# A state-space layer and a routed MLP on one core: statistics made in fours, a copy moved to VectorE, neighbours reordered

## The chip, the cores and the metric

One core of a Trainium2 chip runs one program. The metric is device time in microseconds of one execution; the time of a kernel is the median of its runs. The engines are named as in the profile: PE (TensorE), DVE (VectorE), ACT (ScalarE), POOL (GpSimd), SP (SyncE, which issues most transfers).

## What is computed

`x` is 2048 tokens by 1024, bf16. With `xn` the layer norm of `x`, the output is `x + A(xn) + B(xn)`:

```python
# A: diagonal complex state space, 1024 states
Lam_bar = exp(dt * Lam);  B_bar = ((Lam_bar - 1) / Lam)[:, None] * Bmat
Bu = einsum("bld,pd->blp", x, B_bar)
h = Lam_bar * h + Bu[:, t, :]                 # over all tokens t
y = 2 * einsum("blp,dp->bld", hseq, Cmat).real + x * Dskip
# B: the two tokens with the largest x @ w_r go through a gated MLP (1024 -> 3584 -> 1024)
out = x + scatter_add(zero, idx, ((silu(x_sel @ w_gate) * (x_sel @ w_up)) @ w_down) * sigmoid(r_sel))
```

In A and B, `x` stands for `xn`; B's own `x` is `xn` too. So the output holds `x + xn + Dskip * xn` besides the two products, and as `x = std * xn + mean`, the kernel makes it as `(Dskip + std + 1) * xn + mean`. That is where the standard deviations and means of the title are used.

## The kernel before, in words

The 2048 tokens are cut into 16 chunks of 128, frames of two chunks and superframes of four. A chunk `c` goes through these tasks:

- `x.c` loads it (SP). For chunks 0 to 5 the statistics are `bs.c`, `bn.c` on DVE (L317, L320) and `nmean.c` on POOL; for chunks 6 to 15 `sum.c`, `nmean.c`, `sq.c` on ACT (L326, L357, L332). `rstd.c` on ACT is a logarithm (L283), an Exp for 1/std (L284) and an Exp for std (L286). `apply.c` normalizes, on DVE for chunks 0 to 5 (L346) and on ACT from 6 on (L350). `nmr.c` is minus the mean times 1/std, `nmr1.c` adds one to std (L360 on POOL, L369 on ACT), `mean.c` turns the sign of the negated mean (L363, POOL).
- `Tpe.c` turns the normalized chunk by eight PE transposes (L386, chunks 0 to 3) and `xnT.c` copies it from PSUM (L391 DVE, L393 ACT); from chunk 4 on `T.c` is a transposed transfer.
- `Bu.f.j`, in the first frames split into `Bh.f.j.ri`, multiplies frame `f` by block `j` of B, real and imaginary (L661); `Bs.s.j.ri` does it for a superframe (L672). Block 0 of B is turned by PE (`tB.ri`, L262) and copied by ACT (`B.0.ri`, L265); the others come as transposed transfers (`B.j.ri`, L240). The products go to three PSUM banks in turn, from which ACT evacuates them (`u`, L667; `us`, L680).
- `TI` turns the input by a phase (DVE, L738 to L747), `SC` scans (DVE, L766), `gb` casts the scan (ACT, L772), `cw`, `cy`, `cin` carry the state from chunk to chunk (POOL), `TO` turns back (DVE).
- `xr.c` loads `x` again, `seed.c.dh` puts half `dh` of `xn` into a PSUM bank (ACT, L871), `sk.c.dh` multiplies it by `Dskip + std + 1` (DVE, L881), `Y.c.q` adds the output projection (PE, L891), `ADD.c.dh` adds the mean and evacuates (ACT, L907; DVE for chunk 15, L905), `out.c.dh` stores.
- The MLP: weights by SP (`w.n`), products by PE (`mm.i`), the two rows added to chunk 15's bank by PE where they belong there (`hotY`, L896) and scattered into the output by an indirect transfer (`fix`, L1136).

At the start `warm.i` runs matmuls on the identity (L409, L305) until data is there.

The order of the work is written out by hand: `ORDER` (L25 to L68) lists the tasks, and `Plan.emit` issues them in that order. Each engine then works through its own instructions in order, and waits by semaphores. `Plan.run` only asserts that each task's dependences and buffers stand ahead of it; the durations given to `add` set nothing here.

## Time and profile before

| | us |
|---|---|
| median of 3 runs | 250.15 (250.13 to 250.19) |
| the profiled execution | 250.2 |
| its span, first to last instruction | 248.1 |
| PE busy | 241.1 (97%) |
| DVE busy | 231.0 (93%) |
| ACT busy | 177.4 (71%) |
| POOL busy | 92.1 (37%) |
| mean granted TensorE clock | 0.998 |

The profiled execution is some 2 us longer than its span, for what lies before the first and behind the last instruction. A busy share is an average over the whole span; DMA-issuing instructions are not in it. Rows of a timeline give the start and the busy time; neighbouring instructions of one engine overlap a little, so the start of the next is often before the end of the row above.

### The profile page before, as it was taken

To read this page: it belongs to the slowest core of one execution; us is meant where nothing else is said; L and a number is where in the kernel's file an instruction comes from. 1 tells how busy PE (TensorE), PEld (TensorE's weight loads), DVE (VectorE), ACT (ScalarE), POOL (GpSimd) and SP (SyncE) were. 2 spreads that over 40 slices of the span, in tenths; PEclk is the share of its full clock that TensorE was granted. 3 is DMA by queue.
4 is the path that set the end of the run, shared out by engine and by line. 5 is a ranking of instruction groups with operands and counts; after the bars stand their busy time and mean duration, and the time that the engine had idled before them with its cause. 6 is when DMAs were issued, how large, how long until landed. Compare 5 with 4: busy or idle time off the path is not lost.

```text
span 248.1 us, 4602 instructions
## 1 busy us (share of the span) xinstructions
PE 241.1 (97%) x1723; PEld 139.9 (56%) x1743; DVE 231.0 (93%) x267; ACT 177.4 (71%) x364; POOL 92.1 (37%) x148
## 2 busy tenths in 40 slices
...
GB/s 206 237 190 150 210 171 249 144 274 131 237 144 109 106 97 114 127 3 10 118 184 248 165 0 116 393 225 320 274 176 400 251 376 340 281 202 391 66 64 44
DMA packets 66753, 46.77 MB, mean 189 GB/s; under 512 B 46114, under 2 KB 52648, under 8 KB 66732
## 3 DMA queue, kind: packets, MB, share of 16 engines
...
q8 instruction: 13, 0.21, 0.3%
q10 hardware_dynamic: 192, 0.07, 0.1%
q14 instruction: 8, 0.07, 0.1%
...
## 4 chain that ended last, share of the span: by engine, by line
PE 94%; DMA 2%; issue 1%; DVE 1%; SPq 1%
PE pY L891 44%; PE pB L661 23%; PE pB L672 22%; PE pG L1086 3%; DMA xt<-in_A_x_dram 2%; PE pD L1117 1%; PE r_ps L404 1%; DVE ot L905 1%; PE pT L386 1%; SPq L180 0%; SPq L168 0%; DVE xn L346 0%; SPq L169 0%; PE pY L896 0%; PE pP L474 0%
## 5 line engine op out<-in xcount | busy, mean ns | idle before, releaser
L891 PE MATMUL pY<-CT,hT 128*128 128x512 bf16 (+1 forms) x515 | 113.1, 372 | 0.9 <-issue 0.3
L891 PEld LDWEIGHTS <-hT 128*128 128x128 bf16 x528 | 51.2, 98 | 58.9 <-issue 1.9
L766 DVE TENSOR_TENSOR_SCAN gf<-R,v 128x1040 f32<-128x1040 f32 (+1 forms) x34 | 68.9, 2055 | 1.4 <-POOL v L798 1.0
L782 POOL TENSOR_TENSOR cw<-gf,tL 128x16 f32<-128x16 f32 (+1 forms) x34 | 33.4, 984 | 97.5 <-DVE gf L766 89.8
L672 PE MATMUL pB<-xnT,BT 128*128 128x512 bf16 x249 | 57.0, 379 | 0.4
L661 PE MATMUL pB<-xnT,BT 128*128 128x256 bf16 (+1 forms) x576 | 57.3, 261 | 0.0
L661 PEld LDWEIGHTS <-BT 128*128 128x128 bf16 x576 | 51.1, 98 | 5.6
L907 ACT ACTIVATE ot<-pY,mean_all 128x512 bf16<-128x512 f32 x30 | 20.5, 686 | 33.4 <-PE pY L891 33.2
L672 PEld LDWEIGHTS <-BT 128*128 128x128 bf16 x256 | 24.8, 98 | 30.4 <-PE pG L1086 0.4
L772 ACT CAST gb<-gf 128x1024 bf16<-128x1024 f32 (+1 forms) x34 | 31.8, 940 | 7.5 <-DVE gf L766 7.3
L808 DVE TENSOR_TENSOR m<-gb,E 128x4096 bf16<-128x4096 bf16 x13 | 29.5, 2271 | 0.5 <-ACT gb L772 0.5
L680 ACT CAST u<-pB 128x256 bf16<-128x256 f32 x64 | 19.9, 376 | 10.0 <-PE pB L672 8.0
L871 ACT ACTIVATE pY<-xr,nmr_all,rstd_all 128x512 f32<-128x512 bf16 (+1 forms) x33 | 25.2, 770 | 0.3
L881 DVE SCALAR_TENSOR_TENSOR pY<-Drow,std_all,pY 128x512 f32<-128x512 bf16 (+1 forms) x33 | 23.5, 723 | 0.6 <-ACT pY L871 0.6
L667 ACT CAST u<-pB 128x512 bf16<-128x512 f32 x32 | 18.2, 578 | 2.1 <-PE pB L661 2.0
L810 DVE TENSOR_TENSOR hT<-m 128x2048 bf16<-128x2048 bf16 x13 | 15.9, 1225 | 1.2
L740 DVE TENSOR_TENSOR v<-u,m 128x4096 bf16<-128x4096 bf16 x7 | 16.0, 2292 | 0.2
L738 DVE TENSOR_TENSOR m<-u,E1t 128x4096 bf16<-128x4096 bf16 x7 | 16.0, 2283 | 0.0
L798 POOL TENSOR_TENSOR v<-cy,v 128x16 bf16<-128x16 f32 (+1 forms) x17 | 14.2, 837 | 1.4
L350 ACT ACTIVATE xn<-xt,nmr_all,rstd_all 128x1024 bf16<-128x1024 bf16 x10 | 12.4, 1238 | 0.1
L332 ACT ACTIVATE xn<-xt,nmean_all 128x1024 bf16<-128x1024 bf16 x10 | 11.5, 1153 | 0.1
L797 POOL CAST v<-cy 128x16 bf16<-128x16 f32 (+1 forms) x17 | 10.4, 610 | 0.8
...
## 6 DMA issues: line engine op xcount, KB each, us to landing
...
```

The costliest lines, as they stand in the source:

```text
L661: nc.tensor.matmul(out=pB[:, ri, ts_], lhsT=BT[ri][j][:, k, :], rhs=xnT_frame(f)[:, k, ts_], start=(k == 0), stop=(k == DT - 1))
L667: nc.scalar.copy(out=u_tiles[f][:, :, :, j, :].rearrange("p c i t -> p i c t"), in_=pB_tiles.pop((f, j))[:].rearrange("p i (c t) -> p i c ...
L672: nc.tensor.matmul(out=pB[:], lhsT=BT[ri][j][:, k, :], rhs=xnT_tiles[s][:, k, :], start=(k == 0), stop=(k == DT - 1))
L680: nc.scalar.copy(out=u_tiles[f][:, :, ri, j, :], in_=pB[:, i * TF:(i + 1) * TF].rearrange("p (c t) -> p c t", c=CPF))
L766: nc.vector.tensor_tensor_scan(out=flat(gf), data0=flat(R[:, js, :]), data1=flat(v[:, ri, js, :]), initial=0.0, op0=ALU.mult, op1=ALU.add)
L772: nc.scalar.copy(out=gb_tiles[c][:, ri, js, :], in_=gf_tiles[c, js.start, ri][:, :, 2:])
L782: nc.gpsimd.tensor_tensor(out=cw_tiles[c, js.start][:, ri, :, 0:n], in0=g.unsqueeze(1).to_broadcast([128, 2, n]), in1=tL[:, ri, :, js], op ...
L808: nc.vector.tensor_tensor(out=m[:].rearrange("p k i j t -> p k (i j t)"), in1=E2[:].rearrange("p k i j t -> p k (i j t)"), in0=flat(gb[:]) ...
L871: nc.scalar.activation(out=pY[:, 0:d_.stop - d_.start], in_=y_tiles["xr", c][:, d_], func=ACT.Identity, bias=nmr_all[:, c:c + 1], scale=rs ...
L881: nc.vector.scalar_tensor_tensor(out=pY, in0=ms["Drow"][:, d_], scalar=std1_all[:, c:c + 1], in1=pY, op0=ALU.add, op1=ALU.mult)
L891: nc.tensor.matmul(out=pY, lhsT=h_tiles[c][:, ri, j, :], rhs=CT[ri][h][:, j, d0:d0 + w], start=False, stop=end, skip_group_check=True)
L907: nc.scalar.activation(out=ot, in_=pY, func=ACT.Identity, bias=mean_all[:, c:c + 1])
```

## The change

Three things are changed in the code, and the order besides. The standard deviation is no longer made with each `rstd`: the logarithms are kept in one tile, and `std.g` makes four deviations in one Exp on ACT; `nmr1.g` and `mean.g` are one POOL operation for four chunks each (the additions that ACT did for chunks 6 to 15 go to POOL). `sk` and `ADD` wait for the group's operation. Turned chunk 1 is copied by DVE.

```diff
-    def inv_sqrt(out_ap, var_ap, npart, scale, std=None):
+    def inv_sqrt(out_ap, var_ap, npart, scale):
...
-        if std is not None:
-            nc.scalar.activation(out=std, in_=lv[:npart], func=ACT.Exp, scale=0.5)
...
     def ln_rstd(c, scale):
-        inv_sqrt(rstd_all[:, c:c + 1], ln_part[c][:, 1:2], 128, scale, std1_all[:, c:c + 1])
+        nc.scalar.activation(out=lv_all[:, c:c + 1], in_=ln_part[c][:, 1:2], func=ACT.Ln, bias=eps_t[:], scale=scale)
+        nc.scalar.activation(out=rstd_all[:, c:c + 1], in_=lv_all[:, c:c + 1], func=ACT.Exp, scale=-0.5)
+
+    def ln_std(g):
+        nc.scalar.activation(out=std1_all[:, 4 * g:4 * g + 4], in_=lv_all[:, 4 * g:4 * g + 4], func=ACT.Exp, scale=0.5)
...
-    def ln_std1(c):
-        nc.gpsimd.tensor_scalar_add(out=std1_all[:, c:c + 1], in0=std1_all[:, c:c + 1], scalar1=1.0)
-
-    def ln_mean(c):
-        nc.gpsimd.tensor_scalar_mul(out=mean_all[:, c:c + 1], in0=nmean_all[:, c:c + 1], scalar1=-1.0)
+    def ln_std1(g):
+        nc.gpsimd.tensor_scalar_add(out=std1_all[:, 4 * g:4 * g + 4], in0=std1_all[:, 4 * g:4 * g + 4], scalar1=1.0)
+
+    def ln_mean(g):
+        nc.gpsimd.tensor_scalar_mul(out=mean_all[:, 4 * g:4 * g + 4], in0=nmean_all[:, 4 * g:4 * g + 4], scalar1=-1.0)
...
-    def ln_std1_act(c):
-        nc.scalar.activation(out=std1_all[:, c:c + 1], in_=std1_all[:, c:c + 1], func=ACT.Identity, bias=one_t[:])
...
-    DVE_T = (0,)
+    DVE_T = (0, 1)
...
+    for g in range(NSF):
+        four = range(4 * g, 4 * g + 4)
+        add(("std", g), "ACT", 0.2, lambda g=g: ln_std(g), [("rstd", c) for c in four] + [("log",)], key=4 * g - 24)
+        add(("nmr1", g), "POOL", 0.3, lambda g=g: ln_std1(g), [("std", g)], key=4 * g - 24)
+        add(("mean", g), "POOL", 0.3, lambda g=g: ln_mean(g), [("nmean", c) for c in four], key=4 * g - 24)
```

`ORDER` is another text from its first line on. Two of its first lines, before and after:

```diff
-warm.13 warm.14 tB.0 start.0 nmean.1 x.2 B.1.0 x.3 Tpe.0 Bn.1 B.1.1 B.0.0 xnT.0 bs.2 rstd.1 apply.1 tB.1 Bh.0.0.0 Tpe.1 x.5 bn.2 bs.3 B.0.1 nmean.0
-xnT.1 bn.3 rstd.2 B.2.0 Bh.0.0.1 pP.0 pcol.0 Bh.0.1.0 apply.2 rstd.3 dt frq x.4 B.3.0 B.2.1 Bu.0.0 u.0.0 Bh.0.1.1 Tpe.2 rad Bu.0.1 apply.3 xnT.2 Tpe.3
...
+warm.9 warm.10 warm.11 warm.12 warm.13 warm.14 Tpe.0 xnT.0 Bn.1 x.3 nmean.1 B.1.0 B.1.1 bs.2 apply.1 tB.0 bn.2 tB.1 B.0.0 B.0.1 x.4 Tpe.1 Bh.0.0.0
+B.2.0 B.2.1 B.3.0 rstd.2 xnT.1 bs.3 Bh.0.0.1 pP.0 Bu.0.0 pcol.0 apply.2 x.5 B.3.1 bn.3 dt u.0.0 rstd.3 apply.3 B.4.0 B.4.1 Bh.0.1.0 Tpe.2 Bh.0.1.1
```

Line numbers move by a few: L386 becomes L385, L661 L662, L680 L681, L907 L908.

What PE does at the start, after the last matmul on the identity. Each row is the first matmul of eight; a number behind a name tells buffers apart. Before, with `Bn` the untouched block 0 of B, `xn_185` chunk 0, `xn_240` chunk 1, and `BT0_0`, `BT1_0` the real and imaginary half of block 0:

```order
L262 MATMUL pT_206<-ident_92,Bn_87 128x128
L386 MATMUL pT_221<-ident_92,xn_185 128x128
L262 MATMUL pT_242<-ident_92,Bn_87 128x128
L661 MATMUL pB_251<-xnT_232,BT0_0_115 128x128
L386 MATMUL pT_260<-ident_92,xn_240 128x128
L661 MATMUL pB_251<-xnT_232,BT1_0_123 128x128
L474 MATMUL pP_295<-ident_92,prow_83 128x32
```

After, with `xn_179` chunk 0 and `xn_228` chunk 1:

```order
L385 MATMUL pT_210<-ident_92,xn_179 128x128
L262 MATMUL pT_230<-ident_92,Bn_87 128x128
L262 MATMUL pT_242<-ident_92,Bn_87 128x128
L385 MATMUL pT_255<-ident_92,xn_228 128x128
L662 MATMUL pB_264<-xnT_219,BT0_0_115 128x128
L662 MATMUL pB_264<-xnT_219,BT1_0_123 128x128
L475 MATMUL pP_289<-ident_92,prow_83 128x32
```

Chunk 0 is turned ahead of both halves of B, and the first product stands behind the turn of chunk 1.

VectorE in the same place, from the copy of turned chunk 0 on. Before:

```order
L391 COPY xnT<-pT 128x8x128
L317 BN_STATS st<-xt 128x6
L346 TENSOR_SCALAR xn<-xt,mv,rstd_all 128x1024
L317 BN_STATS st<-xt 128x6
L320 BN_AGGR mv<-st 128x2
L317 BN_STATS st<-xt 128x6 x2
L320 BN_AGGR mv<-st 128x2
L477 CAST pcol<-pP 128x32
L346 TENSOR_SCALAR xn<-xt,mv,rstd_all 128x1024
```

After:

```order
L390 COPY xnT<-pT 128x8x128
L315 BN_STATS st<-xt 128x6
L348 TENSOR_SCALAR xn<-xt,mv,rstd_all 128x1024
L315 BN_STATS st<-xt 128x6
L318 BN_AGGR mv<-st 128x2
L390 COPY xnT<-pT 128x8x128
L315 BN_STATS st<-xt 128x6
L478 CAST pcol<-pP 128x32
L348 TENSOR_SCALAR xn<-xt,mv,rstd_all 128x1024
```

The copy of chunk 1 stands behind the statistics of chunk 2, and one half of chunk 3's statistics goes behind the normalization of chunk 2.

ACT in superframe 2, up to the evacuation of the third group (`us.2.1.0`, the last row of each). Before:

```order
L332 ACTIVATE xn,sm<-xt,nmean_all 128x1024
L357 ACTIVATE nmean_all<-sm 128x1
L871 ACTIVATE pY<-xr,nmr_all,rstd_all 128x512
L283 ACTIVATE lv<-sm,eps_t 128x1
L284 ACTIVATE rstd_all<-lv 128x1
L286 ACTIVATE std_all<-lv 128x1
L680 CAST u<-pB 128x2x128 x2
L871 ACTIVATE pY<-xr,nmr_all,rstd_all 128x512
L680 CAST u<-pB 128x2x128 x2
L907 ACTIVATE ot<-pY,mean_all 128x512
L772 CAST gb<-gf 128x1024
L680 CAST u<-pB 128x2x128 x2
```

After:

```order
L324 ACTIVATE xn,sm<-xt 128x1024
L352 ACTIVATE xn<-xt,nmr_all,rstd_all 128x1024
L681 CAST u<-pB 128x2x128 x2
L872 ACTIVATE pY<-xr,nmr_all,rstd_all 128x512
L773 CAST gb<-gf 128x1024
L681 CAST u<-pB 128x2x128 x2
L773 CAST gb<-gf 128x1024
L908 ACTIVATE ot<-pY,mean_all 128x512
L359 ACTIVATE nmean_all<-sm 128x1
L681 CAST u<-pB 128x2x128 x2
```

The normalization of a chunk (15) and a second cast of the scan now stand ahead of the third evacuation.

## Rows read from the trace of the kernel before

**Rows 1.** The page, part 1: busy us, share of the span, instructions of each engine

```profile
PE 241.1 (97%) x1723; PEld 139.9 (56%) x1743; DVE 231.0 (93%) x267; ACT 177.4 (71%) x364; POOL 92.1 (37%) x148
```

**Rows 2.** PE's waits: line, what it waited for, us in total, times, longest

```profile
PE pT L386 <- DVE xn L346: 0.9, 1, 0.9
PE pT L262 <- DMA Bn<-in_A_B_im_dram: 0.3, 1, 0.3
```

**Rows 3.** PE's timeline: start us, busy us, line, operation, count [idle before it <- releaser]

```profile
1.37 1.89 PE L409 MATMUL warm<-ident 128*128 128x128 bf16 x16 [1.37 <-POOL ident masks.py:199]
...
5.23 0.62 PE L262 MATMUL pT<-ident,Bn 128*128 128x128 bf16 x8
5.74 0.62 PE L386 MATMUL pT<-ident,xn 128*128 128x128 bf16 x8
6.69 0.62 PE L262 MATMUL pT<-ident,Bn 128*128 128x128 bf16 x8 [0.32 <-DMA Bn<-in_A_B_im_dram]
7.14 0.61 PE L661 MATMUL pB<-xnT,BT 128*128 128x128 bf16 x8
8.70 0.62 PE L386 MATMUL pT<-ident,xn 128*128 128x128 bf16 x8 [0.94 <-DVE xn L346]
...
9.81 2.10 PE L661 MATMUL pB<-xnT,BT 128*128 128x128 bf16 x32
11.76 0.61 PE L386 MATMUL pT<-ident,xn 128*128 128x128 bf16 x8
```

**Rows 4.** VectorE's timeline, same columns

```profile
6.45 0.64 DVE L391 COPY xnT<-pT 128x1024 bf16<-128x1024 bf16 x1
7.50 0.69 DVE L317 BATCH_NORM_STATS2 st<-xt 128x6 f32<-128x512 bf16 x1 [0.41 <-DMA xt<-in_A_x_dram]
8.11 0.53 DVE L346 TENSOR_SCALAR xn<-xt,mv,rstd_all 128x1024 bf16<-128x1024 bf16 x1
...
9.28 0.21 DVE L320 BATCH_NORM_AGGREGATE mv<-st 128x2 f32<-128x12 f32 x1
...
11.67 0.17 DVE L486 TENSOR_TENSOR scr<-scr,pcol 128x8 f32<-128x8 f32 x1 [0.28 <-ACT scr L483]
```

**Rows 5.** The chain that ended last: start us, us, the load of chunk 2

```profile
3.08 4.40 DMA xt<-in_A_x_dram
```

**Rows 6.** ACT's timeline, the copy of turned chunk 1

```profile
9.36 1.01 ACT L393 COPY xnT<-pT 128x1024 bf16<-128x1024 bf16 x1 [1.00 <-PE pT L386]
```

**Rows 7.** Groups by line and form: count | busy us, mean ns of one | idle

```profile
L350 ACT ACTIVATE xn<-xt,nmr_all,rstd_all 128x1024 bf16<-128x1024 bf16 x10 | 12.4, 1238 | 0.1
...
L363 POOL TENSOR_SCALAR mean_all<-nmean_all 128x1 f32<-128x1 f32 x15 | 8.5, 574 | 0.0
...
L286 ACT ACTIVATE std_all<-lv 128x1 f32<-128x1 f32 x16 | 3.0, 186 | 0.0
...
L369 ACT ACTIVATE std_all<-std_all,one_t 128x1 f32<-128x1 f32 x10 | 2.7, 289 | 0.0
```

**Rows 8.** Two stretches: length, busy us (count) of PE, PEld, DVE, ACT, POOL; clock; DMA

```profile
75.00:124.00 49.00, 48.74 (x231) 22.86 (x234) 47.69 (x29) 48.37 (x105) 29.38 (x29) 1.00 0.35 87
13.70:244.00 230.30, 229.03 (x1577) 129.82 (x1594) 218.88 (x237) 169.29 (x344) 89.55 (x134) 1.00 0.65 189
```

**Rows 9.** ACT's timeline around 93 us

```profile
93.22 0.68 ACT L680 CAST u<-pB 128x256 bf16<-128x256 f32 x2
93.96 1.04 ACT L772 CAST gb<-gf 128x1024 bf16<-128x1024 f32 x1
```

**Rows 10.** PE's timeline around 97 us

```profile
95.38 1.89 PE L891 MATMUL pY<-CT,hT 128*128 128x512 bf16 x8
97.10 2.10 PE L672 MATMUL pB<-xnT,BT 128*128 128x512 bf16 x8
```

**Rows 11.** The tail on every engine: start us, busy us

```profile
243.54 0.49 PE L896 MATMUL pY<-ymb,hot 128*128 128x512 bf16 x2
...
243.96 1.57 DVE L905 TENSOR_SCALAR ot<-pY,nmean_all 128x512 bf16<-128x512 f32 x3 [3.36 <-PE pY L896]
```

More of the change, by code (lines that the diff above doesn't have):

```diff
@@ new lines @@
+xnT.2 Bu.0.1 frq u.0.1 Tpe.3 rad xnT.3 Bh.1.0.0 Bh.1.1.0 B.5.0 Bh.1.1.1 Bh.1.0.1 turns whole angle trig sin B.5.1 abs first Bu.1.0 u.1.0 Bu.1.1 Bu.1.2
+cos u.1.1 log u.1.2 bs.4 bs.5 sq1.0 bn.5 Bu.0.2 sq1.1 Bu.0.3 Bu.0.4 B.6.0 inv.0 u.0.2 bn.4 rstd.4 B.6.1 rstd.5 inv.1 u.0.3 u.0.4 den rc.0 kappa tan.0
+apply.5 R0.0 apply.4 Bu.1.3 Bu.1.4 nmr.0 Bu.1.5 nmean.2 u.1.3 ntan.0 Bu.0.5 rc.1 R0.1 tan.1 u.1.4 u.1.5 ntan.1 u.0.5 std.0 T.5 x.6 cs TI.0.0 R.1
+nmean.3 cin.0.0 nmr1.0 R.0 ts.0.1 SC.0.0.0 Bu.0.6 Bu.1.6 ts.1.0 sum.6 nmean.6 ts.0.0 sq.6 ends rstd.6 E2c.1 ts.1.1 nmr.6 u.0.6 apply.6 cw.0.0 nmr.1
@@ new lines @@
+out.10.0 seed.12.1 sk.12.1 SC.14.0.0 TO.13.0 out.11.0 xr.14 Y.12.1 mm.5 ADD.11.1 ADD.12.0 out.11.1 gb.14.0.0 seed.13.0 seed.13.1 Y.12.2 Y.12.3 sk.13.0
+SC.14.0.1 sk.13.1 Y.13.0 out.12.0 cw.14.0 cy.14.0 cin.15.0 Y.13.1 Y.13.2 Y.13.3 w.36 w.37 w.38 w.39 w.40 w.41 ADD.12.1 seed.14.0 gb.14.0.1 ADD.13.0
+ADD.13.1 sk.14.0 TO.14.0 Y.14.0 SC.15.6.0 Y.14.1 out.12.1 out.13.1 xr.15 gT.3 SC.15.0.0 SC.15.0.1 mm.6 seed.14.1 sk.14.1 seed.15.0 ADD.14.0 SC.15.4.0
+TO.15.0 out.14.0 rows Y.14.2 Y.14.3 seed.15.1 ADD.14.1 seed.15.2 SC.15.4.1 sk.15.0 TO.15.4 row_.3 sk.15.1 SC.15.6.1 sk.15.2 row_.2 Y.15.0 Y.15.1
@@ L68 @@
+Y.15.2 Y.15.3 Y.15.4 TO.15.6 out.13.0 row_.1 ymb hotY.15.0 Y.15.5 Y.15.6 hotY.15.2 hotY.15.1 ADD.15.0 out.14.1 fix out.15.0 Y.15.7 ADD.15.1 Y.15.8
+out.15.1 ADD.15.2 out.15.2
 """
@@ L221 @@
     mean_all = consts.tile([128, NCH], F32, name="mean_all")
+    lv_all = consts.tile([128, NCH], F32, name="lv_all")
     rad = consts.tile([128, PT], F32, name="rad")
@@ L436 @@
             add(("sq", c), "ACT", 1.15, lambda c=c: ln_sq(c), [("nmean", c)], key=ln)
-            add(("rstd", c), "ACT", 0.77, lambda c=c: ln_rstd(c, 1.0 / D), [("sq", c)] + ([("log",)] if c >= 4 else []), key=ln - 10)
+            add(("rstd", c), "ACT", 0.57, lambda c=c: ln_rstd(c, 1.0 / D), [("sq", c)] + ([("log",)] if c >= 4 else []), key=ln - 10)
             if c in ACT_APPLY:
@@ L444 @@
             add(("nmr", c), "POOL", 0.45, lambda c=c: ln_nmr(c), stat, key=ln + 5)
-            add(("nmr1", c), "POOL", 0.45, lambda c=c: ln_std1(c), stat, key=ln + 5)
         else:
             add(("nmr", c), "ACT", 0.22, lambda c=c: ln_nmr_act(c), stat, key=ln - 10)
-            add(("nmr1", c), "ACT", 0.2, lambda c=c: ln_std1_act(c), stat, key=c - 27)
-        if c < NCH - 1:
-            add(("mean", c), "POOL", 0.2, lambda c=c: ln_mean(c), [("nmean", c)], key=c - 5)
         if c < PE_T:
@@ L923 @@
                 key=c - 24.9, takes=[("pY", (c, dh), [("ADD", c, dh)])])
-            add(("sk", c, dh), "DVE", 0.07 + 1.035e-3 * (d_.stop - d_.start), lambda c=c, dh=dh: skip(c, dh), [("seed", c, dh), ("Drow",), ("nmr1", c)], key=c - 12)
+            add(("sk", c, dh), "DVE", 0.07 + 1.035e-3 * (d_.stop - d_.start), lambda c=c, dh=dh: skip(c, dh), [("seed", c, dh), ("Drow",), ("nmr1", c // 4)], key=c - 12)
         split = len(parts(c)) > 1 and c == NCH - 1
```

73 lines of the change are left out of this document (31 added, 42 removed).

## The prediction, made before the changed kernel was run

> **What bounds the kernel now.** I read the page's busy shares first: TensorE (PE) is busy in 97% of the span, VectorE in 93%, ACT in 71%, POOL in 37% [rows 1]. So time can only come from what PE waits for, and only work that makes PE wait can cost any. PE's waits come next: after its first instruction it waits for a named releaser twice, 0.94 us for the normalized chunk 1 and 0.32 us for a block of B [rows 2]; its timeline puts both between 5 and 9 us [rows 3]. From 13.7 to 244 us PE is busy for 229.03 of 230.30 us [rows 8], and nothing in it is put down to a wait. The tail is last: PE's last matmuls, then three residual adds on VectorE [rows 11]. The change can therefore touch three places: the start up to 12 us, the places in the middle where ACT or VectorE just keeps up, and the tail. The profiled execution took 250.2 us, its span 248.1; the median of the runs is 250.15. I add differences to 250.15. 0.2%, 0.5 us, is about what a measurement of this kernel can tell from no change.
>
> **The start.** Turned chunks 0 and 1 are eight PE transposes each; eight 128-column matmuls take 0.45 us from start to start (6.69 to 7.14 [rows 3]). Before the change PE turns the real half of B while chunk 0 is still being normalized (5.23), and multiplies it by chunk 0 (7.14) while it waits for chunk 1; the wait of 0.94 is what that leaves up to 8.70 [rows 3]. After the change neither fills a wait any more.
> - The turn of B's real half goes behind the turn of chunk 0. That chunk is turned at 5.74 as before, so B's real half at 6.19 and its imaginary half at 6.69 as before: 0.45 us lands in the gap of 0.32 plus what the rows overlap. Nothing. Its copy by ACT moves with it by about 0.9 us, and is needed only after 9.15: nothing.
> - Chunk 1 is turned at 8.70 because VectorE normalizes it at 8.11, behind the first statistics of chunk 2, which start at 7.50 when that chunk has landed [rows 4]; its load was issued at 3.08 and took 4.40 us [rows 5]. The order on VectorE up to there is unchanged, and so is that load's place on SP's queue. So I leave 8.70 where it is. The wait before it then grows from 0.94 to 1.56, less overlap, and the product of chunk 0 with B's real half, 0.45, is done after it: **+0.45**.
> - Given back: the copy of turned chunk 1. ACT takes 1.01 us from 9.36, to 10.37 [rows 6]. In the stretch of 32 matmuls at 9.81 the second eight need it, at 9.81 + 0.45 = 10.26; the stretch lasts 11.76 - 9.81 = 1.95 us where four eights take 1.80 [rows 3]. So 0.15 of it is that wait. With VectorE the copy takes 0.64 [rows 4] and follows the aggregate that ends at 9.28 + 0.21 = 9.49: done at 10.13. PE, now with both halves of B for chunk 0 ahead (8.70 + 3 x 0.45 = 10.05, and a small transpose of 0.1), wants it at 10.16. No wait: -0.15 to **-0.25**.
> - VectorE's 0.64 us more in front of chunk 2's and 3's normalization: chunk 2 is turned when PE is ready for it, at 11.5, and VectorE has it by about 11.2 (10.13, then 0.6 of statistics and 0.5 of normalizing [rows 4]). Soon after, VectorE waits 0.28 us for a table from ACT (11.67 [rows 4]), and ACT has lost a copy of 1.01. Hidden. Without that cover it would cost up to 0.64.
> - On SP the load of chunk 3 goes ahead of the first transposed load of B, and that of chunk 5 behind three more. The first delays a transposed load by one issue of about 0.5 us; its block is now first used an eighth group later than before, near 11.1 instead of 9.81. Nothing.
>
> Net of the start: **+0.2 us**, between +0.45 (nothing given back) and -0.2. The lower end: if chunk 2, with no transposed load right behind it in the queue, lands before 7.09, VectorE loses its idle 0.41 [rows 4], and everything from 8.70 moves up by that: +0.2 - 0.4.
>
> **Statistics in fours.** ACT loses sixteen Exp of 186 ns and ten additions of 289 ns, and gets four Exp on 128x4: 3.0 + 2.7 - 4 x 0.19 = 4.9 us at most. POOL loses fifteen negations (8.5 us) and six additions, and gets eight on 128x4 [rows 7]. The trace has no POOL operation on 128x4 here; bounds are a negation's shortest and longest, and even the mean of 0.574 makes 4.6 for all eight. PE waits for neither engine in these operations: nothing. What is new are waits. The skip add of a chunk now needs all four deviations of its group (behind it on VectorE stand the scans), its residual add all four means (behind it on ACT the evacuations that PE needs). In the new order each group's operations stand ahead of its first user by several matmul groups: the first four chunks are normalized in the first 12 us, and their first skip add follows the first scans. Nothing; if one did wait for a POOL operation, 0.57 us bounds it [rows 7]. On POOL the means of group 1 now stand ahead of the carry of chunk 5: up to 0.57 later, for a scan that VectorE reaches later. Nothing.
>
> **The middle.** ACT is busy for 48.37 of 49.00 us between 75 and 124 us [rows 8]: what the new order puts ahead of an evacuation there arrives at PE. The tight place is superframe 2. Three PSUM banks take the groups of input projection in turn, so the sixth group (second token half of B, output block 2, which starts at 97.10) needs the bank of the third, whose evacuation starts at 93.22 and ends at 93.90 [rows 9, 10]. The new order puts one group of output projection behind that sixth group instead of ahead: PE wants it 97.10 - 95.38 = 1.72 us sooner, at 95.4, or 95.6 with the start's 0.2. On ACT ahead of that evacuation come: the normalization of chunk 15 (+1.24 [rows 7]), a cast of the scan (+1.04 [rows 9]), two Exp in fours (+0.37), less seven single Exp (-1.30 [rows 7]): +1.35 by busy times. Rows overlap their neighbours by up to 0.1, and so taken apart it is +1.6. The evacuation ends at 93.90 + 0.2 + (1.35 to 1.6) = 95.45 to 95.7, where PE wants 95.6. I take **+0.1 us**, with 0 and 0.9 as ends: nothing if ACT's idle 0.63 of that stretch [rows 8] absorbs it; 0.9 if the next two groups, behind a square pass as long as that normalization, are late by 0.3 to 0.4 each as well. The other moves there I reckoned alike and leave at nothing.
>
> **The tail.** The product that adds the routed rows to chunk 15's first half stands at 243.54, with eight 256-column matmuls behind it [rows 11]; it moves ahead of four groups, but that half's last group now ends eight matmuls before PE's end, as it did. VectorE's three adds (1.57 us [rows 11]) start at the same distance from PE's end within 0.1 us: **-0.1 to 0**, taken as -0.1.
>
> **Sum:** 250.15 + 0.2 + 0 + 0.1 - 0.1 = 250.35, **250.4 us**.
>
> **The rivals.**
> 1. *ACT becomes the bound in superframe 2* (ends on the other side). Place: the evacuation at 93.22. It decides as soon as the work ahead of it grows by more than 1.5 us (95.6 less 0.2 less 93.90). For: ACT has 0.63 us free in 49 [rows 8]. Against: 4.9 us less to do by then at most. Price 0.9 less the 0.1 counted: about 251.1.
> 2. *Chunk 2 lands early*: the start gains 0.2 instead of losing 0.2. For: it waits 4.40 us for a transfer [rows 5]. Against: its place in the queue is the same. 249.95.
> 3. *The clock falls in the longer wait.* The first sixteen matmuls took 1.89 us, 118 ns each, and the eights from 5.23 on 0.45 to 0.5, under 65 ns [rows 3]: the lower of the two levels (1.2 GHz), then the higher (2.4 GHz). The granted clock stayed high through waits of 0.32 and 0.94, with 24 of the 32 matmuls from 5.23 to 8.70 transposes [rows 3]. After the change that stretch holds only transposes, and waits of 0.5 and 1.5. If the clock fell at 8.7 and took as long to rise as at the start (1.37 to at most 5.23, 3.9 us at half speed), PE would lose 1.9 us: 252.3.
>    The Trainium skill, "TensorE: Matmul & The Clock Gate", on PE transposes, says of that mode that "it doesn't count as PE-busy the same way"; by that the stretch would not hold the clock, which speaks against this change; the trace so far shows the clock held by transposes with eight ordinary matmuls among them, so it decides nothing for a stretch without any.
> 4. *The middle tightens.* PE's 1.27 us outside its busy time between 13.7 and 244 [rows 8] have no releaser; if the new order takes most of it back, 0.8 us, the time is 249.5. For: neighbours are moved throughout. Against: matmul ends are modelled, so this may be no idle time at all.
>
> **How the numbers follow.** Forecast 0.50, ACT late 0.25, early landing 0.12, clock 0.05, tighter middle 0.08. The forecast's own range, 250.2 to 250.8, passes 250.65 one time in ten. Same: 0.45 + 0.12 = 0.57; slower: 0.05 + 0.25 + 0.05 = 0.35; faster: 0.08. The range runs from the early landing, 249.9, to ACT late, 251.2; the clock, the tighter middle and a little of ACT's case are left out.
>
> **What would show it.** Right: PE turns chunk 1 at 8.6 to 8.8 with a wait near 1.5 us before it, chunk 2 at about 11.5, one named wait more at most, on ACT's evacuation near 95 us, under 0.3 us. The start is wrong if chunk 1 is turned before 8.4; the middle, if PE's waits name ACT or VectorE for over 0.5 us in all; the clock, if eights behind 8.7 us take 0.9 us. A time below 249.6 or above 251.2 would make the prediction wrong.

## The result, and the profile after

| | before | after |
|---|---|---|
| median, us (6 runs each) | 250.14 (249.69 to 250.62) | 251.94 (251.79 to 252.15) |
| profiled execution / span, us | 250.2 / 248.1 | 252.15 / 250.3 |
| last matmul of PE starts, us | 244.74 | 245.59 |
| last store is issued, us | 245.56 | 247.18 |
| span ends, us | 248.09 | 250.34 |

The ratio is 1.0072 [1.0059, 1.0085]: 1.8 us slower, above the range of the prediction. The profiled execution of after is the slowest of its six, and the time outside the span is 2.1 us in before's profiled execution and 1.8 in after's; so the parts of the span add up to more than the medians' 1.8 us. Why the outside is shorter, no run shows. The last three rows divide the span's 2.25 us: PE is 0.85 later at its last matmul; the last store follows that matmul after 1.59 us instead of 0.82 (+0.77); the span ends 3.16 us after the last store's issue instead of 2.53 (+0.63).

The page, part 1, of after (beside [rows 1]): ACT has lost 3.5 us, VectorE gained 1.0, and PE's 0.8 more hold no more matmuls.

```profile
PE 241.9 (97%) x1722; PEld 140.5 (56%) x1743; DVE 232.0 (93%) x268; ACT 173.9 (69%) x341; POOL 92.5 (37%) x135
```

PE's waits of after (beside [rows 2]), without the one for the identity, which either kernel has:

```profile
PE pT L385 <- DVE xn L348: 1.2, 2, 0.8
PE pY L892 <- DVE pY L882: 0.2, 1, 0.2
```

The second row is new, and names VectorE's skip add, not ACT's evacuation. **The start**, PE's timeline of after (beside [rows 3]):

```profile
4.33 1.06 PE L408 MATMUL warm<-ident 128*128 128x128 bf16 x8
5.78 1.03 PE L385 MATMUL pT<-ident,xn 128*128 128x128 bf16 x8 [0.39 <-DVE xn L348]
6.60 1.20 PE L262 MATMUL pT<-ident,Bn 128*128 128x128 bf16 x16
8.64 0.62 PE L385 MATMUL pT<-ident,xn 128*128 128x128 bf16 x8 [0.84 <-DVE xn L348]
9.10 1.06 PE L662 MATMUL pB<-xnT,BT 128*128 128x128 bf16 x16
...
11.56 0.61 PE L385 MATMUL pT<-ident,xn 128*128 128x128 bf16 x8
...
13.34 0.61 PE L385 MATMUL pT<-ident,xn 128*128 128x128 bf16 x8
```

Chunk 1 is turned at 8.64, chunk 2 at 11.56, and chunk 3 at 13.34, where before had 13.10: +0.24. The eight transposes at 8.64 are followed after 0.46 us, so the clock was at its higher level there. Those of chunk 0 at 5.78 took 0.82 us to the next start, where before the eights from 5.23 on took 0.45 to 0.51. The trace's record of the granted clock begins at 4.92 us in before and at 6.88 in after, and just there the starts of PE's 128-column matmuls go from 107 ns apart to 56: the lower level (1.2 GHz) up to there, the higher (2.4 GHz) behind. In after the clock rose only among the transposes of B, in before among the last matmuls on the identity. This is not the order's doing: in all profiles but one, which is told of below, the rise lies anywhere from 4.17 to 7.14 us, in either order.

What differs between executions as well is when VectorE can start on chunk 2: at 7.05 to 7.76 us, in either order and with the same exception (7.50 before, 7.46 after). Counted from there, chunk 3 is turned 5.58 to 5.60 us later in the seven profiles with the first tasks of before, and 5.88 to 5.90 in eight with those of after. So the new start costs 0.30 us; the +0.24 is this less 0.04 of an earlier landing.

**The middle.** Both kernels give PE the same matmuls in another order, so I compare the times at which PE had equally many columns behind it. Counted so, after is 0.25 us behind from 13 to 95 us, 0.46 from there to 182, 0.85 from 185 to PE's end; one row of the chain of either kernel shows the last. The chain of before, then of after (start us, us, what):

```profile
195.29 1.41 PE pG L1086 x24
```

```profile
196.14 1.41 PE pG L1087 x24
```

The step of 0.20 at 95 us is superframe 2: the evacuation that the prediction reckoned to end at 95.45 to 95.7 ends at 95.14 + 0.65 = 95.79, ACT's timeline of after:

```profile
95.14 0.65 ACT L681 CAST u<-pB 128x256 bf16<-128x256 f32 x2
```

The step of 0.39 is at 182 us. VectorE's timeline of after, then PE's, then PE's of before:

```profile
178.22 1.23 DVE L811 TENSOR_TENSOR hT<-m 128x2048 bf16<-128x2048 bf16 x1
179.36 2.32 DVE L767 TENSOR_TENSOR_SCAN gf<-R,v 128x1040 f32<-128x1040 f32 x1
181.60 0.73 DVE L882 SCALAR_TENSOR_TENSOR pY<-Drow,std_all,pY 128x512 f32<-128x512 bf16 x1
```

```profile
182.38 1.89 PE L892 MATMUL pY<-CT,hT 128*128 128x512 bf16 x7 [0.23 <-DVE pY L882]
184.20 1.48 PE L1087 MATMUL pG<-wt,mw 128*32 128x512 bf16 x24
```

```profile
175.70 5.99 PE L672 MATMUL pB<-xnT,BT 128*128 128x512 bf16 x26
181.62 1.48 PE L1086 MATMUL pG<-wt,mw 128*32 128x512 bf16 x24
```

The wait that the view names (0.23) is less than the step, because the modelled end of the matmul ahead of it runs on. In after the second scan of chunk 11 (`SC.11.0.1`, 2.32 us) stands ahead of the skip add of chunk 9, and PE has the projection `Y.9.0`, which needs that add, ahead of the MLP's `mm.2`, which does not. Before, PE ran `mm.2` there.

**The tail.** ACT, SP, POOL and VectorE in after's timelines:

```profile
230.68 0.78 ACT L872 ACTIVATE pY<-xr,nmr_all,rstd_all 128x512 f32<-128x512 bf16 x1
234.90 0.78 ACT L872 ACTIVATE pY<-xr,nmr_all,rstd_all 128x512 f32<-128x512 bf16 x1 [3.44 <-DMA xr<-in_A_x_dram]
235.62 0.67 ACT L908 ACTIVATE ot<-pY,mean_all 128x512 bf16<-128x512 f32 x1
236.19 0.45 ACT L1130 ACTIVATE ymb<-pD,sig 2x256 bf16<-2x256 f32 x1
```

```profile
223.90 7.26 SPq L912 DMA_DIRECT2D out_dram<-ot  x2
231.22 1.46 SPq L866 DMA_DIRECT2D xr<-in_A_x_dram  x1
```

```profile
243.67 1.41 POOL L1137 DMA_INDIRECT out_dram<-ymb,idx_t  x1 [17.58 <-issue]
```

```profile
244.81 1.57 DVE L906 TENSOR_SCALAR ot<-pY,nmean_all 128x512 bf16<-128x512 f32 x3 [3.17 <-PE pY L892]
```

The same places in before (SP, ACT, POOL):

```profile
227.50 0.46 SPq L865 DMA_DIRECT2D xr<-in_A_x_dram  x1
```

```profile
234.53 0.45 ACT L1129 ACTIVATE ymb<-pD,sig 2x256 bf16<-2x256 f32 x1
```

```profile
242.06 1.42 POOL L1136 DMA_INDIRECT out_dram<-ymb,idx_t  x1 [17.66 <-issue]
```

The load of `x` for chunk 15's seed (`xr.15`) now stands on SP behind a store that waits for its residual add (`out.13.1`), and is issued at 231.22 instead of 227.50. ACT waits 3.44 us for it; behind that seed on ACT stand the rows of the MLP's result (236.19 instead of 234.53), behind them the scattered store (243.67 instead of 242.06), and behind that `out.15.0`, which starts 2.73 us later, at 246.40; the last store follows it on SP at 247.18. In before `out.15.0` went out at 244.91, 2.85 after the scatter, and the last store then waited for the last of VectorE's adds (done at 245.53). Here those adds are done at 246.38, and the last store has no wait for them.

**The close.** The transfers in the 1.6 us after the last store's issue (queue: packets, MB, share of 16 engines), of before and of after:

```profile
q1 hardware_dynamic: 288, 0.20, 37.9%
q10 hardware_dynamic: 144, 0.07, 14.1%
```

```profile
q1 hardware_dynamic: 288, 0.20, 38.7%
q10 hardware_dynamic: 144, 0.07, 14.8%
q14 instruction: 1, 0.01, 1.4%
```

The same stores go; in after one packet of the queue that loads instructions (8 KB) is among them, 0.85 us after the last store's issue. In before it comes at 1.62, when they have landed. The packet took 0.35 us; behind it the last packets of the stores follow one another up to 1.39, where in before the last of them starts at 1.19, and the last store lands at 2.02 instead of 1.61. SP's last wait for a store's landing ends 2.03 us after that issue instead of 1.62, and VectorE's closing drain (one of its last steps) comes 0.38 us after SP's instead of 0.03: 0.41 + 0.35 = 0.76, of which 0.63 arrives at the span's end.

### The profile page after: what moved, and what is told of

Same layout as the page of the kernel before. It is cut to its first block, busy times and chain, and to the rows that moved or that the text cites. A ratio compares the mean times of both kernels' runs of the same rounds, so it can differ in the third digit from the quotient of the medians.

```text
span 250.3 us, 4574 instructions
## 1 busy us (share of the span) xinstructions
PE 241.9 (97%) x1722; PEld 140.5 (56%) x1743; DVE 232.0 (93%) x268; ACT 173.9 (69%) x341; POOL 92.5 (37%) x135
## 5 line engine op out<-in xcount | busy, mean ns | idle before, releaser
L783 POOL TENSOR_TENSOR cw<-gf,tL 128x16 f32<-128x16 f32 (+1 forms) x34 | 35.0, 1030 | 96.0 <-DVE gf L767 95.7
L662 PE MATMUL pB<-xnT,BT 128*128 128x256 bf16 (+1 forms) x576 | 57.2, 261 | 0.0
L662 PEld LDWEIGHTS <-BT 128*128 128x128 bf16 x576 | 51.0, 98 | 5.7
L908 ACT ACTIVATE ot<-pY,mean_all 128x512 bf16<-128x512 f32 x30 | 20.4, 684 | 35.7 <-PE pY L892 32.5
L681 ACT CAST u<-pB 128x256 bf16<-128x256 f32 x64 | 20.3, 377 | 8.4 <-PE pB L673 8.2
L798 POOL CAST v<-cy 128x16 bf16<-128x16 f32 (+1 forms) x17 | 12.3, 721 | 1.0
L330 ACT ACTIVATE xn<-xt,nmean_all 128x1024 bf16<-128x1024 bf16 x10 | 11.5, 1152 | 0.1
L791 POOL TENSOR_TENSOR cy<-cw 128x16 f32<-128x16 f32 (+1 forms) x17 | 11.0, 648 | 1.3
```

The costliest lines, as they stand in the source:

```text
L662: nc.tensor.matmul(out=pB[:, ri, ts_], lhsT=BT[ri][j][:, k, :], rhs=xnT_frame(f)[:, k, ts_], start=(k == 0), stop=(k == DT - 1))
L681: nc.scalar.copy(out=u_tiles[f][:, :, ri, j, :], in_=pB[:, i * TF:(i + 1) * TF].rearrange("p (c t) -> p c t", c=CPF))
L783: nc.gpsimd.tensor_tensor(out=cw_tiles[c, js.start][:, ri, :, 0:n], in0=g.unsqueeze(1).to_broadcast([128, 2, n]), in1=tL[:, ri, :, js], op ...
L908: nc.scalar.activation(out=ot, in_=pY, func=ACT.Identity, bias=mean_all[:, c:c + 1])
```

## The experiments

**The changed kernel again**, beside the second set below:

> The changed kernel once more, unaltered, on the chip of the three kernels beside it. Both theories: 251.8 to 252.2 us. Theory (four places): PE 0.25 us behind the kernel before after the turn of chunk 3, give or take 0.3 for the landing of the first loads, and 0.2 and 0.39 us more behind at 95 and 182 us; the indirect store near 243.7.

251.76 (12 runs), ratio 1.0062 [1.0040, 1.0083]: just under the expected range, and the result stands. The parts differ from the first profile: PE ends 0.73 us late, the scatter starts at 243.26 instead of near 243.7, the last store follows PE after 1.29 us (+0.47, not +0.77), and the close is 3.26. From the issue of `xr.15` to the seed that reads it it took 3.68 us in the first profile of after and 3.38 here, so the price of the tail is not the same in each execution.

### First set: undo one place at a time

**`a1_xr15`**, the load back ahead of the store:

```diff
-out.12.1 out.13.1 xr.15 gT.3
+out.12.1 xr.15 out.13.1 gT.3
```

> The changed kernel, with the load of chunk 15 for its residual issued ahead of the second store of chunk 13 instead of behind it. Theory (four places): in the changed kernel that load waits for a store that waits for PE; so ACT's seed of chunk 15 waits 3.44 us, the routed rows behind it are made 1.24 us later than PE has them, the indirect store starts at 243.67 instead of about 242.4, and the last stores, which wait for its landing, go out late. Expected: ACT's wait of 3.44 us gone, indirect store at 242.3 to 242.6, PE's last matmuls where they were, time lower by 0.75 to 1.3 us: 250.6 to 251.2. Rival (the tail only follows PE, and its extra 1.3 us is chance): the indirect store moves, the time stays within 0.2 us of 251.9.

251.29, 1.0046 [1.0032, 1.0059], where after had 1.0072 and, again, 1.0062. SP's timeline, then ACT's:

```profile
223.93 0.42 SPq L866 DMA_DIRECT2D xr<-in_A_x_dram  x1
```

```profile
232.01 0.78 ACT L872 ACTIVATE pY<-xr,nmr_all,rstd_all 128x512 f32<-128x512 bf16 x1 [0.94 <-DMA xr<-in_A_x_dram]
...
234.59 0.46 ACT L1130 ACTIVATE ymb<-pD,sig 2x256 bf16<-2x256 f32 x1 [0.74 <-PE pD L1118]
```

The wait falls from 3.44 to 0.94, the rows wait for PE, the scatter is back at 242.08 and the last store at 0.82 us after the last matmul, as before the change. One moved load is what the tail's loss came from; 0.5 to 0.65 us shows in the medians, a little less than expected. PE ends 0.47 us late in this profile, not 0.85, because chunk 2 happened to land early (VectorE starts on it at 7.11). The close stays long (3.38 us).

**`a2_start`**, the first hundred tasks in the order of before, chunk 1 copied by ACT:

```diff
-    DVE_T = (0, 1)
+    DVE_T = (0,)
```

> The changed kernel, with the first tasks, up to the turn of chunk 3, in the order of the kernel before, and turned chunk 1 copied by ACT again. Theory (four places): PE reaches the turn of chunk 3 0.25 us earlier and stays 0.25 us earlier to the end; the load of chunk 15 follows, so time 251.6 to 251.8. Rival (the start's loss is taken back by a wait further on): PE's lead of 0.25 is gone by its last matmul, time unchanged within 0.1.

252.10, 1.0070 [1.0056, 1.0084]. In its profile PE ends 0.60 us late instead of 0.85, and that execution took 251.47; the others took 252.0 to 252.2. The start's 0.25 is seen at PE, not in the time, and the expected 251.6 to 251.8 is missed: inconclusive. The time outside the span is 2.1 to 2.2 us in its executions and 1.8 in those of after, which would hide such a gain; why, is open.

**`a3_scan`**, the scan of chunk 11 and what hangs on it behind the skip adds, all engines:

```diff
-TO.10.0 SC.11.0.1 cw.11.0 cy.11.0 gb.11.0.1 sk.9.0 gT.0 sk.8.1 hot
+TO.10.0 sk.9.0 gT.0 sk.8.1 SC.11.0.1 cw.11.0 cy.11.0 gb.11.0.1 hot
```

> The changed kernel, with the second scan of chunk 11 (2.3 us on VectorE) and what hangs on it behind the skip adds of chunks 9 and 8 and the turn of the MLP's block 0, instead of ahead of them. Theory (four places): PE no longer waits for the skip add near 182 us; 0.39 us back, 251.4 to 251.7, and no new wait. Rival (VectorE is so full there that the wait only moves): PE waits for a scan or a turn of chunk 11 or 12 before 195 us instead, time within 0.15 us of 251.9.

253.39, 1.0124 [1.0108, 1.0139]: slower than after. The wait at 182 is gone, and others come, PE's timeline:

```profile
199.24 7.07 PE L892 MATMUL pY<-CT,hT 128*128 128x512 bf16 x32 [0.22 <-DVE pY L882]
...
223.32 10.04 PE L892 MATMUL pY<-CT,hT 128*128 128x512 bf16 x44 [0.15 <-DVE pY L882]
```

PE ends 1.35 us late. PE now waits for the skip adds of later chunks. That fits the rival's cause, a VectorE that is full there, but not its size: the rival had the time unchanged, and the waits stand behind 195 us. Why the median lies another 0.7 us above the profiled execution (252.65) stays open.

**`a4_four`**, these three and `apply.15` behind `us.2.1.1`:

```diff
-sum.12 apply.15 us.2.0.0 cw.3.0
+sum.12 us.2.0.0 cw.3.0
-us.2.1.1 rstd.12
+us.2.1.1 apply.15 rstd.12
```

> The changed kernel with all four places undone: the load of chunk 15 as in the first, the start as in the second, the scan as in the third, and the normalization of chunk 15 behind the evacuations of superframe 2's third and fourth groups. The statistics stay in fours, the rest of the new order stays. Theory (four places): nothing of the loss is left, 249.9 to 250.4, PE's last matmuls within 0.1 us of the kernel before. Rival (the statistics in fours cost by themselves, by their waits or on POOL): 0.5 us or more stay, 250.7 or above.

253.24, 1.0117 [1.0101, 1.0132], 3 us above what was expected. PE's timeline, then ACT's:

```profile
119.18 1.90 PE L892 MATMUL pY<-CT,hT 128*128 128x512 bf16 x8 [0.46 <-DVE hT L811]
...
200.60 7.07 PE L892 MATMUL pY<-CT,hT 128*128 128x512 bf16 x32 [0.70 <-DVE pY L882]
```

```profile
101.58 1.06 ACT L324 ACTIVATE xn<-xt 128x1024 bf16<-128x1024 bf16 x1 [2.51 <-DMA xnT<-xn]
```

With chunk 15 normalized later, its transposed transfer frees a buffer later; ACT waits 2.51 us for it and PE loses 1.1 us between 105 and 119. So these moves of work on ACT and VectorE did not undo two of the four places. What the statistics in fours cost, this run can't tell; the next one does.

### Second set: one part of the change alone

**`b2_stats`**, the order and ACT's copy of before, the statistics in fours:

```diff
-            add(("nmr1", c), "POOL", 0.45, lambda c=c: ln_std1(c), stat, key=ln + 5)
...
+    for g in range(NSF):
+        four = range(4 * g, 4 * g + 4)
+        add(("std", g), "ACT", 0.2, lambda g=g: ln_std(g), [("rstd", c) for c in four] + [("log",)], key=4 * g - 24)
```

> The kernel before in its own order, turned chunk 1 copied by ACT, with only the statistics in fours: each group's Exp and its two POOL operations stand where one of the four stood. Theory (the order cost the time, the fours nothing): 250.0 to 250.5 us, no new wait of PE. Rival (the fours cost by their waits or on POOL): 250.8 or above.

250.36, 0.9985 [0.9957, 1.0013]. The fours cost at most 0.3 us, and in the profile nothing: PE has no new wait, and the rival in which a skip add waits for its group falls. PE ends 0.25 us earlier than in before, as much as VectorE starts earlier on chunk 2 (7.25): two executions with the same first tasks differ by that much.

**`b3_copy`**, before with the copy of chunk 1 by VectorE:

```diff
-    DVE_T = (0,)
+    DVE_T = (0, 1)
```

> The kernel before with only one thing changed: VectorE copies turned chunk 1. By the rows of before VectorE then has the copy at 10.04, both statistics of chunk 3 until 11.35 and chunk 2 normalized at 11.95, where PE without a wait would want it at 11.5: PE turns chunk 2 at about 12.0 instead of 11.76 with a wait near 0.45 in front. Theory (VectorE's order, not the copy's length, decides there): 250.3 to 250.6. Rival (the shorter copy is a gain by itself, 0.15 us): 249.9 to 250.1.

250.51, 1.0008 [0.9988, 1.0029]. PE's timeline:

```profile
10.77 1.50 PE L661 MATMUL pB<-xnT,BT 128*128 128x128 bf16 x24 [0.25 <-DVE xnT L391]
12.12 0.62 PE L386 MATMUL pT<-ident,xn 128*128 128x128 bf16 x8
```

In the order of before the copy stands behind half of chunk 3's statistics, and chunk 2 is turned at 12.12 instead of 11.76; PE ends 0.38 late. The median is as the theory had it, but the interval holds both theory and rival: too little for the time to show.

**`c1_pe`**, `xr.15` as in `a1_xr15`, and the two waits of the middle undone on PE alone:

```diff
-w.17 Y.9.0 mm.2 Y.8.0
+w.17 mm.2 Y.9.0 Y.8.0
-TO.4.0 Bs.2.2.1 out.2.1
+TO.4.0 Y.3.0 Bs.2.2.1 out.2.1
-gb.5.0.1 Y.3.0 Y.3.1
+gb.5.0.1 Y.3.1
```

> The changed kernel with the load of chunk 15 ahead of the second store of chunk 13, and two moves on PE alone: the MLP's third group of products ahead of the first projection of chunk 9 instead of behind it, and the first projection group of chunk 3 ahead of the sixth input group of superframe 2 instead of behind it, as in the kernel before. VectorE, ACT and POOL keep the new order. Theory (PE asked 1.4 us and 1.7 us too early at these two places; nothing there has to be faster): PE's waits at 95 and 182 us are gone and do not come back, PE ends 0.25 us behind the kernel before, time 250.3 to 250.7. Rival (VectorE is full there, as the run with the moved scan suggests): a wait of 0.3 us or more for a skip add comes back before 200 us, 250.9 or above.

251.15, 1.0042 [1.0016, 1.0068], above the expected 250.3 to 250.7. Asking later on PE does what moving the work did not: the waits at 95 and 182 are gone, none comes back before 200 us, and some 0.2 us do near 225. In the medians this is 0.14 beside `a1_xr15`, less than the profile lets expect, with intervals that overlap. In its profiled execution (252.4) a load of the start landed late, VectorE's timeline:

```profile
5.25 0.69 DVE L315 BATCH_NORM_STATS2 st<-xt 128x6 f32<-128x512 bf16 x1 [0.79 <-DMA xt<-in_A_x_dram]
```

The clock, too, rose only at 10.22 us, so the turn of chunk 1 (from 9.32) ran at the lower level and took 0.82 us where it took 0.46 in after. Together they make everything behind 1.1 us later, so I read its waits and its median, not its span. The close is 3.47 us.

### Third set: the close, and the copy once more

**`d1_before_pad`**, before with four idle loads of 32 bytes on SP near 95 us:

```diff
-Bs.2.6.1 out.2.1 gb.6.0.1
+Bs.2.6.1 out.2.1 pad.0 pad.1 pad.2 pad.3 gb.6.0.1
...
+        add(("pad", i), "SP", 0.4, lambda t=pad_t: nc.sync.dma_start(out=t[:], in_=A_Dskip.unsqueeze(0)[0:1, 0:16]), key=0)
```

> The kernel before with four idle loads of 32 bytes more on SP, near 95 us, where nothing waits for SP. In every profile of the new order the chip's load of instructions (8 KB on its own queue) comes 0.6 to 0.9 us behind the issue of the last store and the last stores take 0.35 to 0.65 us longer to land; in those of the old order it comes 1.6 us behind it, when they have landed. SP has 215 records in the old order and 220 in the new, by waits that its order needs. Theory (SP's instruction count places that load): the four move it to 0.4 to 1.1 us behind the last store, the last stores land 0.2 to 0.6 us later, time 250.4 to 250.9. Rival (the landing depends on something else in the tail): as the kernel before, within 0.15 us.

250.54, 1.0007 [0.9985, 1.0028]. The instruction load moves from 1.62 to 1.33 us after the last store's issue, so SP's count does place it, though not as far as expected. SP's last closing wait moves from 1.62 to 1.91, and the close is 0.28 longer in the profile. But that is not a later landing: the last store lands at 1.64, in before at 1.61. At its end SP waits for the semaphores of the transfers (the counters that they raise on landing) one after another, in the same order in each run, and one that is already raised takes it 0.06 to 0.07 us. The last store of before raises the semaphore that is waited for last; with four more transfers it raises one with four waits behind it. The time doesn't separate it.

**`d2_c1_pad`** and **`d3_c1_padv`**, `c1_pe` with ten such loads there, the second also with eight fills on VectorE:

```diff
-out.2.1 out.1.0 T.15
+out.2.1 pad.0 pad.1 pad.2 pad.3 pad.4 pad.5 pad.6 pad.7 pad.8 pad.9 out.1.0 T.15
```

> The changed kernel with the earlier load of chunk 15 and the two moves on PE, and ten idle loads of 32 bytes more on SP near 95 us. Theory (SP's instruction count places the load of instructions): ten move it ahead of the last stores, into SP's wait for the indirect store; the last stores land as in the kernel before, and 0.4 to 0.65 us of that kernel's 251.15 go: 250.5 to 250.8. Rival: no change, 251.0 to 251.3.

> The same, and eight one-column fills more on VectorE in its 3 us of idle time ahead of the last residual adds. With 321 records VectorE's last drain comes 0.35 us later than with 315 to 317. Theory (VectorE's count places a load of its own instructions in the closing steps): that goes too, 250.1 to 250.5. Rival: the fills change nothing, as the kernel with the ten loads alone within 0.15 us.

252.82, 1.0084 [1.0059, 1.0109], and 253.53, 1.0119 [1.0092, 1.0146]. The edit was flawed, and the mistake is that of the change itself: the pads stand on SP ahead of chunk 15's transposed transfer. ACT's timeline of the first:

```profile
102.46 1.06 ACT L324 ACTIVATE xn<-xt 128x1024 bf16<-128x1024 bf16 x1 [3.97 <-DMA xnT<-xn]
```

PE loses 2 us there, and the times say nothing of the close. The profiles do: the instruction load comes at 1.14 us in the first, and not among the last stores in the second, and the last store lands at 1.62 and 1.59, as in before. Both have VectorE's drain back at 0.03 us after SP's, the first without any fill, so it is not the fills alone that set it.

**`d4_copy2`**, before with VectorE's copy right behind `bn.2`, half of chunk 3's statistics behind `apply.2`:

```diff
-bn.2 bs.3 B.0.1 nmean.0
-xnT.1 bn.3 rstd.2
+bn.2 xnT.1 bs.3 B.0.1 nmean.0
+rstd.2
-apply.2 rstd.3
+apply.2 bn.3 rstd.3
-    DVE_T = (0,)
+    DVE_T = (0, 1)
```

> The kernel before with turned chunk 1 copied by VectorE right behind chunk 2's statistics, and the second half of chunk 3's statistics behind the normalization of chunk 2. Theory (with the copy on VectorE its order decides): chunk 2 is turned near 11.5 instead of 11.76 us, chunk 3 within 0.1 of the 13.10 of before, because chunk 3's statistics are later now; time 250.0 to 250.4, 0.2 us or more below the kernel with the copy alone. Rival (the copy's 0.64 us on VectorE cost whatever the order): 250.45 or above.

251.10, 1.0032 [1.0016, 1.0049]. PE's timeline, then VectorE's:

```profile
11.50 0.61 PE L386 MATMUL pT<-ident,xn 128*128 128x128 bf16 x8
...
13.46 0.62 PE L386 MATMUL pT<-ident,xn 128*128 128x128 bf16 x8 [0.47 <-DVE xn L346]
```

```profile
12.71 0.17 DVE L486 TENSOR_TENSOR scr<-scr,pcol 128x8 f32<-128x8 f32 x1 [0.79 <-ACT scr L483]
```

Chunk 2 is turned at 11.50, but chunk 3 is late, PE ends 0.66 late, and VectorE's wait for ACT's table doesn't shrink but grows. My theory that the copy hides in front of that table falls and the rival holds: in this order, too, VectorE's 0.64 us costs about as much.

### Fourth set: everything undone that was found

Each is `c1_pe` with more undone. **`e1_fills`**: eight one-column fills on VectorE behind `TO.15.6`. **`e2_start`**: these, and the start of `a2_start`. **`e3_sp`**: the fills and ten idle loads on SP behind `xr.15`, where SP waits anyway. **`e4_all`**: all of it.

```diff
-TO.15.6 out.13.0
+TO.15.6 padv.0 padv.1 padv.2 padv.3 padv.4 padv.5 padv.6 padv.7 out.13.0
...
+        add(("padv", i), "DVE", 0.06, lambda i=i: nc.vector.memset(padv[:], 0.0), key=0)
```

> The changed kernel with the earlier load of chunk 15 and the two moves on PE (251.15 us), and eight one-column fills on VectorE in its idle time ahead of the last residual adds; SP as it was. Theory (the closing step waits for VectorE's own load of instructions): VectorE's last drain comes 0.3 to 0.4 us earlier against the last store, 250.7 to 250.95. Rival (that delay came with something else that the ten loads on SP altered): 251.0 to 251.3.

> The same with the fills, and the first tasks in the order of the kernel before, turned chunk 1 copied by ACT. Theory (the start costs 0.25 us by itself and nothing downstream takes it back): 0.15 to 0.35 below the kernel with the fills alone, 250.4 to 250.8. Rival (VectorE, not the start, sets PE's pace later): equal within 0.1.

> The kernel with the fills, and ten idle loads of 32 bytes on SP behind the load of chunk 15, where SP waits for a store's data for some 6 us; nothing stands behind them that is wanted sooner. Theory (the last stores share their transfer engines with SP's load of instructions): that load comes ahead of the last stores, the last one lands 1.6 to 1.9 us after its issue instead of 2.0 to 2.3, 0.2 to 0.5 below the kernel with the fills: 250.3 to 250.7. Rival (the landing depends on the order of the tail's stores): within 0.1 of the kernel with the fills.

> All of it: statistics in fours, the new order with the earlier load of chunk 15 and the two moves on PE, the start of before with ACT's copy, eight fills, ten idle loads. Theory (all five places are found): 250.0 to 250.5, as the kernel before. Rival (something of the new order costs beside them): 250.6 or above.

| | median, us | ratio to before | end after last store's issue, us |
|---|---|---|---|
| before | 250.28 | | 2.53 (first profile) |
| `c1_pe` (second set) | 251.15 | 1.0042 [1.0016, 1.0068] | 3.47 |
| `e1_fills` | 251.23 | 1.0033 [1.0020, 1.0046] | 3.30 |
| `e2_start` | 251.04 | 1.0035 [1.0021, 1.0048] | 3.22 |
| `e3_sp` | 250.97 | 1.0023 [1.0002, 1.0045] | 2.89 |
| `e4_all` | 250.55 | 1.0011 [1.0000, 1.0023] | 2.89 |

Transfers in the 1.6 us after the last store's issue, in `e1_fills` and in `e3_sp`:

```profile
q1 hardware_dynamic: 279, 0.19, 38.2%
q10 hardware_dynamic: 144, 0.07, 14.6%
q14 instruction: 1, 0.01, 2.2%
```

```profile
q1 hardware_dynamic: 288, 0.20, 39.9%
q10 hardware_dynamic: 144, 0.07, 15.0%
```

With the idle loads no instruction load falls among the last stores, and all 288 packets of their queue are sent in that stretch instead of 279. The last store lands at 1.60 us, as in before, instead of 2.37: this load cost the landing 0.77 us. Only 0.40 of it shows at SP's last wait (1.99 instead of 2.39), because the ten loads also move the last store to the semaphore that SP waits for first. SP's waits for landings at the end (us in total, times, longest), of before and of `e3_sp`:

```profile
SPq L1194 <- DMA out_dram<-ot: 0.9, 3, 0.5
```

```profile
SPq L1202 <- DMA out_dram<-ot: 1.3, 1, 1.3
```

In `e3_sp` SP waits once, up to 1.62 us after the issue, and then steps through six semaphores that are already raised, up to 1.99. So the 0.35 us by which the close of the last two rows is longer than before's is what the ten idle loads add themselves.

All eighteen profiles agree with this. In nine the instruction load comes 0.56 to 0.88 us after the last store's issue, and that store lands at 1.96 to 2.37. In the other nine, of either order, it comes at 1.14 or later or not among the last stores, and the landing is at 1.59 to 1.64. SP has 215 records in before, 219 in `d1_before_pad`, 220 in the new order and 221 in `a4_four`, and the load comes at 1.62, 1.33, 0.77 to 0.88 and 0.56: the more records SP has, the earlier it comes, and the five more of the new order (all of them waits) brought it among the stores.

The fills alone take VectorE's drain from 0.38 to 0.03 us behind SP's, and the time does not fall: the rival of `e1_fills` holds. The start of before is worth 0.19 us (`e2_start` beside `e1_fills`) and 0.42 (`e4_all` beside `e3_sp`) in the medians, around the 0.30 of the profiles. With all of it, 250.55 lies 0.3 us above before, between what theory and rival had; PE ends 0.29 late, of which 0.2 came behind 195 us. The five places hold nearly all of the loss. No version is shown to beat the kernel before.

## Why the prediction was wrong

The sum rested on one sentence: "only work that makes PE wait can cost any". It failed: 1.40 of the span's 2.25 us lie behind PE's last matmul, where the tail was put at -0.1 and the close was no term.

- **The start** was right: +0.25 against +0.2, chunk 1 at 8.64 (8.6 to 8.8), chunk 2 at 11.56 (about 11.5). The mechanism is there as well: the product of 0.45 stands behind the wait, and the 0.15 that PE waited for ACT's copy is gone, which makes the 0.30 above; that the landing gave 0.04 back is luck. The wait before chunk 1 is 0.84, not near 1.5, because the clock rose only at 6.88: the turn of chunk 0 took 0.82 us instead of 0.45, and B's two halves filled PE to 7.80 (6.60 + 1.20), time that lies ahead of a wait and costs nothing. The lesser bet in it, "Hidden" for VectorE's 0.64, holds only with the new start: `b3_copy` and `d4_copy2` put PE 0.38 and 0.66 behind.
- **Statistics in fours** at nothing: right as far as `b2_stats` can tell, within 0.3 us.
- **Superframe 2**, +0.1: +0.20, within its ends. The place and the mechanism were right, as the step goes when PE asks later (`c1_pe`), and ACT's rival at its price of 0.9 did not come.
- **"The other moves there I reckoned alike and leave at nothing"** failed: +0.39 at 182 us. I looked at ACT, which is tight from 75 to 124 us, and not at VectorE, which is full nearly throughout, for what its new order puts ahead of a skip add. Two orders had to be read together: a scan ahead of the add on VectorE, and the group that needs it ahead of one that does not on PE.
- **"The tail", -0.1,** failed by the most: +0.77. I took PE's and VectorE's order there, and reckoned the adds' distance from PE's end. SP's queue I checked only at the start; in the tail a load was moved past a store that waits. `a1_xr15` shows it: one swap puts the last store back to 0.82 us after the last matmul. The size varies: +0.47 in the second profile of after, +0.25 and +0.83 in those of `a2_start` and `a3_scan`, which keep that order.
- **The close**, +0.63, was no term at all: I took what lies behind the last store as fixed. Of it 0.41 is a later landing, tied to an instruction load among the last stores: it is there in all nine profiles where that load comes within 0.9 us of the issue and in none of the others, and `e3_sp` takes both away. The rest goes with VectorE's closing drain, 0.35 later; what sets that drain stays open, and taking it away (`e1_fills`) did not lower the time. What the landing is worth in the time is less sure: 0.26 between the medians of `e1_fills` and `e3_sp`, whose intervals overlap.
- **The rivals**: none happened. The clock did not fall behind 8.7: the eights at 8.64, with nothing but transposes since 5.78, ran at the higher of the two levels (0.46 us, 56 ns from start to start). The slow eight at 5.78 is no form of that rival: the clock had not yet risen. The prediction's 118 ns for the first matmuls is busy time by count; from start to start they are 107 ns apart. Chunk 2 did not land early in after, though it does in some executions of either order. The middle did not tighten. The rival on the other side was sought at ACT alone.

Sum of the right and missed terms: 0.25 + 0.20 + 0.39 + 0.77 + 0.63 = 2.24, the span's difference in the two profiled executions. They are the span of one execution each, not the 1.8 us between the medians.
